# Moving operands whose places go round modulo 512 bytes: attention and two MLPs on one core

## The chip, the cores and the metric

The kernel runs on 1 core of a Trainium2 chip. The metric is the time of one execution on the device in microseconds; the kernel before has a median of 899.9 us over 3 runs (899.09 to 900.56).

## The reference

Attention over 4 batches, 8 heads, 576 positions of 64 elements, with a local mask (32 positions back) for heads 0 to 3 and a strided mask (every 32nd position) for heads 4 to 7, and then two MLPs over the 2304 tokens with 512 features and 2048 hidden ones. In short:

```
scores = q @ k.T / 8, masked;  attn = softmax(scores);  o = attn @ v
x = o as (2304, 512)
for w_in (512, 2048), w_out (2048, 512) of two layers:
    h = maximum(x @ w_in, 0)
    x = (h * h) @ w_out
```

All inputs and outputs are float32.

## The kernel before

**Operands in two parts.** TensorE multiplies in its fast float32 format. So every large operand is split into a high part and a rest (`hi` written by ScalarE, `lo = src - hi` by VectorE), and a product is made of three matmuls: hi by hi, hi by lo, lo by hi. Weights arrive as 64-bit words and are converted on VectorE and ScalarE while the first layer runs; attention's small matmuls are spread between those of the first three blocks.

**Blocks and steps.** The tokens of a layer are cut in five blocks (`BLOCKS`): four of 512 tokens (wide) and one of 256 (narrow). The narrow one is the fourth of the first layer and the first of the second. A step `s` takes one block and 128 hidden features (`f`), or two times 128 for a narrow block. So the first layer has 72 steps, of which 48 to 55 are narrow, and the second has 72, of which 72 to 79 are narrow. In step `s` TensorE runs the first product of step s+1 (`mm1`, line 704) and then the second product of step `s` (`mm2`, line 766, or for wide blocks of the second layer `products`, line 889).

**Which operand moves.** A matmul holds one operand still (stationary, loaded by a weight load) and streams the other through (moving, up to 512 columns).
- `mm1` (L704): w_in is stationary, x moves: 12 matmuls of 512 columns in a wide step, 24 of 256 in a narrow one. x of a block lies in the tiles `xh` and `xl`, four rows `c` of 512 floats each.
- `mm2` of the first layer (L766): w_out is stationary, g = relu(h) squared moves, from the tiles `gh` and `gl`: 12 matmuls of 512 columns or 24 of 256. In the narrow block of the second layer g is stationary and w_out moves, 12 matmuls of 512 columns.
- `products` (L889), wide blocks of the second layer: seven Strassen products over 256-wide halves. A pair of steps (f even and f odd) works on one set of operands. Combinations of g are stationary (`gah`, `gal`, `gbh`, `gbl`), combinations of w_out move, 256 columns each. The latter lie in a ring over the free x tiles, seven halves of 256 floats, which `w_operands` writes: first three (`PA`), then four (`PB`). A pair has 18 matmuls of the first three and 24 of the other four.

**Where they lie.** In the built program's layout the tiles of x, of the weights and of g (moving and stationary) all begin 128 bytes past a multiple of 512; the tile `gap` is there to bring this about. In this text a place is an operand's distance from that, modulo 512 bytes. Before the change every moving operand of L704 is at place 0, that of L766 at place 0 for wide blocks and 192 (48 floats) for the first layer's narrow block, that of L889 at 192.

**What sets the order.** The program is recorded in the order in which the code calls its operations (`manual_schedule`); each engine runs its own list in that order and waits on semaphores for the others.

Of the kernel before, what the change touches and what calls it, by code (L numbers as in the profile page):

```python
# [16 lines left out]
P = 128  # L17
B, H, S, D = 4, 8, 576, 64
STRIDE = 32
# [6 lines left out]
TB = 512  # L26
# [34 lines left out]
HALF = DM // 2  # L61
# [82 lines left out]
def r32(ap):  # L144
    return ap.bitcast(F32)
# [3 lines left out]
def tile_attention_then_two_mlps(  # L149
# [139 lines left out]
    def ready(key):  # L289
        while key not in wt:  # L290
            conv_by(1)
        return wt[key]
# [227 lines left out]
    def one_small():  # L520
        if small:
            small.pop(0)()
# [21 lines left out]
    def turn_x(i):  # L544
# [3 lines left out]
        for g in range(ng):  # L548
# [3 lines left out]
                ident[:nq, :nq],  # L552
            )

    def x_parts(i):

        b, u, kind, f = fills[i]
        ps = x_ps[i]
        parts = []
        if kind == "l":  # L560
            c = u
            t0, t1 = b * S + f * LQ, b * S + (f + 1) * LQ
            for j, (b0, nb) in enumerate(BLOCKS[0]):
                lo, hi = max(t0, b0), min(t1, b0 + nb)
                if lo < hi:
                    parts.append((j, ps[:, lo - t0:hi - t0], lambda x, a=lo - b0, e=hi - b0: x[:, c, a:e]))
        else:
            c = 2 + u
            r0, n, ng = SFILLS[f]
            n *= ng  # L570
            src = ps[:, :n * NPOS].rearrange("p (r i) -> p i r", i=NPOS)
            i0 = b * NPOS
            for j, (b0, nb) in enumerate(BLOCKS[0]):
                b0, nb = b0 // STRIDE, nb // STRIDE
                lo, hi = max(i0, b0), min(i0 + NPOS, b0 + nb)
                if lo < hi:
                    parts.append((
                        j,
                        src[:, lo - i0:hi - i0],
                        lambda x, a=lo - b0, e=hi - b0: x[:, c].rearrange(  # L580
                            "p (i r) -> p i r", r=STRIDE)[:, a:e, r0:r0 + n],
                    ))
        return parts
# [69 lines left out]
    blocks = [(layer, j) for layer in range(2) for j in range(NB)]  # L653

    def tiles_of(k):
        layer, j = blocks[k]
        return TB // BLOCKS[layer][j][1]
# [3 lines left out]
    xin = {}  # L661
# [9 lines left out]
    def split_y(k, c):  # L671
        layer, j = blocks[k]
        n = BLOCKS[layer][j][1]
        h, lo = (x[:, c, :n] for x in xin[k])
        t = y_in.pop((k, c))[:, :n]
        nc.scalar.activation(out=h, in_=t, func=AF.Copy)
        nc.vector.tensor_tensor(out=lo, in0=t, in1=r32(h), op=ALU.subtract)
# [3 lines left out]
    def block_x(k):  # L681
        layer, j = blocks[k]
        return (xh[j], xl[j]) if layer == 0 else xin[k]

    def mm1(s, point):

        if s >= len(steps):
            return
        k, f = steps[s]
        ne = tiles_of(k)  # L690
        n = TB // ne
        x_hi, x_lo = block_x(k)
        if s == first_7 + 1 or s != 1 and s < first_7 and n_att[0] == len(att):
            ps = ps_a.tile([P, TB], F32, tag="a", name="ps_h")
        elif s != 1:
            ps = ps_h.tile([P, TB], F32, tag="h", name="ps_h")
        else:
            ps = ps_a.tile([P, TB], F32, tag="a", name="ps_h")
        for c in range(KC):
            for e in range(ne):  # L700
                w = ready(("in", blocks[k][0], f + e))
                for i, (a, x) in enumerate(((0, x_hi), (0, x_lo), (1, x_hi))):

                    nc.tensor.matmul(  # L704
                        ps[:, e * n:(e + 1) * n],
                        lhsT=w[:, a, c * P:(c + 1) * P],
                        rhs=x[:, c, :n],
                        start=c == 0 and e == 0 and i == 0,
                        stop=c == KC - 1 and i == 2 and e == ne - 1,
                    )  # L710
                    one_small()
            if c < KC - 1:
                point()
        if s >= first_7:
            t = sqs[s] = gpool.tile([P, TB], F32, tag=("r", "sq")[s % 2], name="sq", bufs=1)
            nc.scalar.activation(out=t, in_=ps, func=AF.Relu, scale=W_BACK)  # L716
            nc.vector.tensor_tensor(out=t, in0=t, in1=t, op=ALU.mult)  # L717
            return

        g0 = 48 if ne > 1 and blocks[k][0] == 0 else 0  # L720
        r = gpool.tile([P, TB], F32, tag="r", name="r", bufs=1)
        sq = gpool.tile([P, TB], F32, tag="sq", name="sq", bufs=1)
        nc.scalar.activation(out=r, in_=ps, func=AF.Relu, scale=W_BACK)  # L723
        h = gpool.tile([P, TB + P], F32R, tag="gh", name="gh", bufs=2)[:, g0:g0 + TB]
        lo = gpool.tile([P, 3 * HALF], F32R, tag="gl", name="gl", bufs=2)[:, g0:g0 + TB]
        if 0 < n_load[0] - n_part[0]:

            nc.scalar.activation(out=sq, in_=r, func=AF.Square)
            nc.scalar.activation(out=h, in_=sq, func=AF.Copy)  # L729
        else:  # L730
            nc.scalar.activation(out=h, in_=r, func=AF.Square)
            nc.vector.tensor_tensor(out=sq, in0=r, in1=r, op=ALU.mult)  # L732
        nc.vector.tensor_tensor(out=lo, in0=sq, in1=r32(h), op=ALU.subtract)  # L733
        gh[s], gl[s] = h, lo
# [57 lines left out]
    sqs, ga, gb, w_parts, rings, banks = {}, {}, {}, {}, {}, {}  # L792
# [3 lines left out]
    def ring(n):  # L796

        if n not in rings:
            rings[n] = [x_tile(t, n).rearrange("p c n -> p (c n)") for t in ("xh", "xl")]
        return rings[n]  # L800
# [14 lines left out]
    def w_operands(s, first):  # L815

        k, f = steps[s]
        n = 1 if k == len(blocks) - 1 and f % 4 == 1 else 2
        wr = w_parts[s] = [x[:, 48:48 + 7 * HALF] for x in ring(n)]
        w = ready(("out", 1, f - 1)), ready(("out", 1, f))  # L820
        src, a, e = (w[0][:, 0:3], 0, 3) if first else (w[1], 3, 7)
        hi, lo = (x[:, a * HALF:e * HALF] for x in wr)
        parts(hi, lo, src.rearrange("p i m -> p (i m)"))

    def quarters(s):
# [43 lines left out]
    def products(s, which, point):  # L869
        k, f = steps[s]  # L870
        nt = TB // 2 // P
        first, end = f == 1, f == NF - 1
        wr = w_parts[s]
        (h, lo), names, w0 = (ga.pop(s), PA, 0) if which == 0 else (gb.pop(s), PB, 3)
        if first:
            tags = ("y0", "y1", "y2") if which == 0 else ("y3", "a", "a", "a")
            for name, tag in zip(names, tags):
                pool = ps_a if tag == "a" else ps_y
                banks[name] = pool.tile([P, 512], F32, tag=tag, name="ps_y")

        at = ((0, 2, 1) if first else (0, 1, 2)) if which == 0 else (2, 0, 3, 1)
        for i in at:
            y = banks[names[i]]
            cols = slice((w0 + i) * HALF, (w0 + i + 1) * HALF)
            for t in range(nt):
                rows = slice(t * P, (t + 1) * P)
                for m, (a, w) in enumerate(((h, wr[0]), (h, wr[1]), (lo, wr[0]))):

                    nc.tensor.matmul(  # L889
                        y[:, t * HALF:(t + 1) * HALF],  # L890
                        lhsT=a[:, i, rows],
                        rhs=w[:, cols],
                        start=first and t == 0 and m == 0,
                        stop=end and t == nt - 1 and m == 2,
                    )
            point()
            if end:
                sums(k, names[i])
# [65 lines left out]
    first = {k: steps.index((k, 0)) for k in range(NB, 2 * NB)}  # L964
    y_at = {}
    for k, s in first.items():

        s, lag, each = (first[NB], 2, 1) if k == NB + 1 else (s - 12, 3, 2)
# [7 lines left out]
    with tc.manual_schedule():  # L976
# [3 lines left out]
        ps = ps_h.tile([P, TB], F32, tag="h", name="ps_w")[:, :P]  # L980
# [18 lines left out]
        for s in range(len(steps)):  # L999
            k, f = steps[s]  # L1000
            layer, j = blocks[k]
# [5 lines left out]
            def point(s=s, layer=layer, j=j, f=f):  # L1007
                n_pt[0] += 1
                at = N_PT * s + n_pt[0]
                for b, (p0, p1) in enumerate(spans):  # L1010
                    if at > p0:
                        lo, hi = att_end[b], att_end[b + 1]
                        att_to(min(hi, lo + -(-(hi - lo) * (at - p0) // (p1 - p0))))
                if n_part[0] < half1:
                    conv_by(1 if n_pt[0] % 4 else 2)
                elif j == NB - 1 and f > 2 and layer == 0 or layer == 1 and n_pt[0] % 4:
                    conv_by(1)
# [3 lines left out]
            if s != first_7:  # L1021
                mm1(s + 1, point)
# [47 lines left out]
```

## Time and profile before

| | |
|---|---|
| median of 3 runs | 899.9 us |
| lowest, highest | 899.09, 900.56 us |
| span of the profiled execution | 896.8 us |
| granted TensorE clock, mean over the span | 0.993 |
| TensorE busy | 876.6 us (98%) in 5216 matmul instructions |
| weight loads busy | 765.4 us (85%) |
| VectorE busy | 631.2 us (70%) |
| ScalarE busy | 491.5 us (55%) |

The span runs from the first to the last instruction; the time of a run also holds what lies around it. Matmuls are pipelined: each is recorded from its start until its last result is written, which overlaps the next ones. How closely they follow each other is read from the chain of waits in order of time, where consecutive matmuls of one line are merged into a piece: its length divided by its count is the spacing. By stage: attention fills the first 40 us alone; the first layer's blocks run from 41 to 155, 157 to 266, 268 to 373, 375 to 418 (narrow) and 420 to 505 us; the second layer's from 507 to 550 (narrow), 552 to 631, 633 to 715, 717 to 799 and 801 to 883 us (Strassen), and a tail ends at 896.8.

### The profile page before, as it was taken

To read this page: it belongs to the slowest core of one execution; us is meant where nothing else is said; L and a number is where in the kernel's file an instruction comes from. 1 tells how busy PE (TensorE), PEld (TensorE's weight loads), DVE (VectorE), ACT (ScalarE), POOL (GpSimd) and SP (SyncE) were. 2 spreads that over 40 slices of the span, in tenths; PEclk is the share of its full clock that TensorE was granted. 3 is DMA by queue.
4 is the path that set the end of the run, shared out by engine and by line. 5 is a ranking of instruction groups with operands and counts; after the bars stand their busy time and mean duration, and the time that the engine had idled before them with its cause. 6 is when DMAs were issued, how large, how long until landed. Compare 5 with 4: busy or idle time off the path is not lost.

```text
span 896.8 us, 14022 instructions
## 1 busy us (share of the span) xinstructions
PE 876.6 (98%) x5216; PEld 765.4 (85%) x5216; DVE 631.2 (70%) x1521; ACT 491.5 (55%) x987; POOL 0.2 (0%) x4
## 2 busy tenths in 40 slices
PE   9699999999999999999999999999999999999997
PEld 8578878888888888899888898899989989998996
DVE  6999973477665665322299996777777787778676
ACT  6787863455555454322377794555545555554443
POOL 0000000000000000000000000000000000000000
PEclk9799999999999999999999999999999999999999
DMA  8956510222222220010566530100010020001001
GB/s 258 344 197 216 196 42 19 86 76 72 88 76 82 75 65 12 1 48 5 184 201 204 179 121 1 48 12 13 18 55 24 1 72 1 24 1 48 1 1 48
DMA packets 45939, 72.00 MB, mean 80 GB/s; under 512 B 3504, under 2 KB 32304, under 8 KB 45872
## 3 DMA queue, kind: packets, MB, share of 16 engines
q1 hardware_dynamic: 45872, 71.12, 24.0%
q8 instruction: 41, 0.67, 0.3%
q14 instruction: 26, 0.21, 0.1%
HBM read 61.67 MB, written 9.44 MB: 79 GB/s over the span
## 4 chain that ended last, share of the span: by engine, by line
PE 82%; DVE 14%; issue 2%; ACT 2%; DVEq 0%; ACTq 0%
PE ps_h L704 39%; PE ps_y L766 21%; PE ps_y L889 15%; DVE raw L223 2%; PE ps_o L503 2%; DVE val L234 2%; DVE w L268 2%; PE ps_pt L487 1%; DVE o L909 1%; PE ps_s L351 1%; DVE raw L220 1%; DVE s L464 1%; PE ps_s L444 1%; DVE gl L733 1%; PE ps_x L549 1%
## 5 line engine op out<-in xcount | busy, mean ns | idle before, releaser
L704 PE MATMUL ps_h<-xh,w 128*128 128x512 f32 (+1 forms) x1280 | 401.9, 374 | 0.0
L704 PEld LDWEIGHTS ps_h<-xh,w 128*128 128x128 f32 x1280 | 234.0, 189 | 36.2
L704 PE MATMUL ps_h<-xl,w 128*128 128x512 f32 (+1 forms) x640 | 236.4, 369 | 0.0
L766 PE MATMUL ps_y<-gh,w 128*128 128x512 f32 (+1 forms) x640 | 157.5, 376 | 0.0
L704 PEld LDWEIGHTS ps_h<-xl,w 128*128 128x128 f32 x640 | 121.3, 189 | 15.0 <-DVE xl L591 0.2
L766 PEld LDWEIGHTS ps_y<-gh,w 128*128 128x128 f32 x640 | 108.0, 188 | 16.5 <-ACT gh L729 0.2
L723 ACT ACTIVATE r<-ps_h 128x512 f32<-128x512 f32 x80 | 47.7, 596 | 122.4 <-PE ps_h L704 85.2
L732 DVE TENSOR_TENSOR sq<-r 128x512 f32<-128x512 f32 x50 | 34.6, 692 | 103.3 <-ACT r L723 103.3
L831 DVE TENSOR_TENSOR xl<-wf,xh 128x768 fp32r<-128x768 f32 (+1 forms) x80 | 80.0, 1010 | 18.5 <-ACT xh L830 18.2
L766 PE MATMUL ps_y<-gl,w 128*128 128x512 f32 (+1 forms) x320 | 85.4, 374 | 0.0
L830 ACT ACTIVATE xh<-wf 128x768 fp32r<-128x768 f32 (+1 forms) x80 | 68.9, 880 | 25.2 <-PE ps_y L889 25.2
L717 DVE TENSOR_TENSOR sq<-sq 128x512 f32<-128x512 f32 x64 | 44.1, 689 | 53.4 <-ACT sq L716 53.4
L716 ACT ACTIVATE sq<-ps_h 128x512 f32<-128x512 f32 x64 | 37.9, 593 | 72.5 <-PE ps_h L704 69.3
L889 PE MATMUL ps_y<-xl,gbh 128*128 128x256 f32 x256 | 72.1, 282 | 0.9 <-DVE xl L831 0.9
L889 PE MATMUL ps_y<-xh,gbl 128*128 128x256 f32 x256 | 71.9, 281 | 0.2 <-DVE gbl L831 0.2
L889 PE MATMUL ps_y<-xh,gbh 128*128 128x256 f32 x256 | 71.8, 281 | 0.0
L733 DVE TENSOR_TENSOR gl<-sq,gh 128x512 fp32r<-128x512 f32 x80 | 55.3, 691 | 20.5 <-ACT gh L729 14.6
L766 PEld LDWEIGHTS ps_y<-gl,w 128*128 128x128 f32 x320 | 54.5, 188 | 8.6
L480 ACT ACTIVATE s<-s,m 96x128 f32<-96x128 f32 (+2 forms) x176 | 55.7, 387 | 5.4 <-DVE m L464 4.8
L889 PE MATMUL ps_y<-xl,gah 128*128 128x256 f32 x192 | 54.0, 281 | 0.2 <-DVE xl L831 0.2
L889 PE MATMUL ps_y<-xh,gah 128*128 128x256 f32 x192 | 54.2, 282 | 0.0
L889 PE MATMUL ps_y<-xh,gal 128*128 128x256 f32 x192 | 54.0, 281 | 0.0
(77 smaller groups left out, 1347.2 us busy)
## 6 DMA issues: line engine op xcount, KB each, us to landing
raw<-moe_w_in_d SPq DMA_DIRECT2D x32, 512.0 KB, 4.7
raw<-moe_w_out_d SPq DMA_DIRECT2D x32, 512.0 KB, 3.8
qk<-loc_qk_d SPq DMA_DIRECT2D x12, 416.0 KB, 3.1
out_d<-o SPq DMA_DIRECT2D x18, 256.0 KB, 2.4
y_dram<-o SPq DMA_DIRECT2D x16, 256.0 KB, 2.1
y_in<-y_dram SPq DMA_DIRECT2D x16, 256.0 KB, 3.0
qk<-loc_qk_d SPq DMA_DIRECT2D x12, 304.0 KB, 3.6
v<-loc_v_d SPq DMA_DIRECT2D x24, 130.0 KB, 2.7
```

What stands on the lines that cost most here:

```text
L223: nc.vector.scalar_tensor_tensor(out=lower, in0=upper, scalar=-(2 ** 31), in1=lower, op0=ALU.bitwise_and, op1=ALU.bitwise_or)
L480: nc.scalar.activation(out=blk, in_=blk, func=AF.Exp, scale=-1.0, bias=m[:nq, j:j + 1])
L704: nc.tensor.matmul(ps[:, e * n:(e + 1) * n], lhsT=w[:, a, c * P:(c + 1) * P], rhs=x[:, c, :n], start=c == 0 and e == 0 and i == 0, stop=c ...
L716: nc.scalar.activation(out=t, in_=ps, func=AF.Relu, scale=W_BACK)
L717: nc.vector.tensor_tensor(out=t, in0=t, in1=t, op=ALU.mult)
L723: nc.scalar.activation(out=r, in_=ps, func=AF.Relu, scale=W_BACK)
L732: nc.vector.tensor_tensor(out=sq, in0=r, in1=r, op=ALU.mult)
L733: nc.vector.tensor_tensor(out=lo, in0=sq, in1=r32(h), op=ALU.subtract)
L766: nc.tensor.matmul(y, lhsT=lhsT, rhs=rhs, start=f == 0 and c not in seen, stop=end and m == last[c])
L830: nc.scalar.activation(out=hi, in_=src, func=AF.Copy)
L831: nc.vector.tensor_tensor(out=lo, in0=src, in1=r32(hi), op=ALU.subtract)
L889: nc.tensor.matmul(y[:, t * HALF:(t + 1) * HALF], lhsT=a[:, i, rows], rhs=w[:, cols], start=first and t == 0 and m == 0, stop=end and t == ...
```

## The change

The moving operands get other starting places inside their tiles. `x_at` gives each of the four rows of a narrow block's x a shift of its own: 0, 64, 96 and 128 floats in the first layer, 16, 32, 80 and 112 in the second (wide blocks fill their rows and stay). g of step `s` begins 16 x (s modulo 8) floats into its tile in both layers before the Strassen blocks, where it began at 48 for the first layer's narrow block and at 0 elsewhere. Strassen's operands of w_out begin at 16 x (s // 2 modulo 8) floats for the pair of step `s`, where they began at 48; their last four halves lie 128 floats further on than the first three would have them, which leaves the place modulo 512 bytes as it is. 16 floats are 64 bytes, so eight shifts go once round 512 bytes. The changed kernel issues the same instructions in the same order on every engine, with the same waits; starting addresses alone differ.

```diff
--- before.py
+++ after.py
@@ -552,6 +552,12 @@
                 ident[:nq, :nq],
             )
 
+    def x_at(layer, n, c):
+
+        if n == TB:
+            return 0
+        return ((0, 64, 96, 128), (16, 32, 80, 112))[layer][c]
+
     def x_parts(i):
 
         b, u, kind, f = fills[i]
@@ -563,7 +569,7 @@
             for j, (b0, nb) in enumerate(BLOCKS[0]):
                 lo, hi = max(t0, b0), min(t1, b0 + nb)
                 if lo < hi:
-                    parts.append((j, ps[:, lo - t0:hi - t0], lambda x, a=lo - b0, e=hi - b0: x[:, c, a:e]))
+                    parts.append((j, ps[:, lo - t0:hi - t0], lambda x, a=lo - b0, e=hi - b0, o=x_at(0, nb, c): x[:, c, o + a:o + e]))
         else:
             c = 2 + u
             r0, n, ng = SFILLS[f]
@@ -571,13 +577,14 @@
             src = ps[:, :n * NPOS].rearrange("p (r i) -> p i r", i=NPOS)
             i0 = b * NPOS
             for j, (b0, nb) in enumerate(BLOCKS[0]):
+                o = x_at(0, nb, c)
                 b0, nb = b0 // STRIDE, nb // STRIDE
                 lo, hi = max(i0, b0), min(i0 + NPOS, b0 + nb)
                 if lo < hi:
                     parts.append((
                         j,
                         src[:, lo - i0:hi - i0],
-                        lambda x, a=lo - b0, e=hi - b0: x[:, c].rearrange(
+                        lambda x, a=lo - b0, e=hi - b0, o=o, nb=nb: x[:, c, o:o + nb * STRIDE].rearrange(
                             "p (i r) -> p i r", r=STRIDE)[:, a:e, r0:r0 + n],
                     ))
         return parts
@@ -671,7 +678,8 @@
     def split_y(k, c):
         layer, j = blocks[k]
         n = BLOCKS[layer][j][1]
-        h, lo = (x[:, c, :n] for x in xin[k])
+        o = x_at(layer, n, c)
+        h, lo = (x[:, c, o:o + n] for x in xin[k])
         t = y_in.pop((k, c))[:, :n]
         nc.scalar.activation(out=h, in_=t, func=AF.Copy)
         nc.vector.tensor_tensor(out=lo, in0=t, in1=r32(h), op=ALU.subtract)
@@ -697,6 +705,7 @@
         else:
             ps = ps_a.tile([P, TB], F32, tag="a", name="ps_h")
         for c in range(KC):
+            x0 = x_at(blocks[k][0], n, c)
             for e in range(ne):
                 w = ready(("in", blocks[k][0], f + e))
                 for i, (a, x) in enumerate(((0, x_hi), (0, x_lo), (1, x_hi))):
@@ -704,7 +713,7 @@
                     nc.tensor.matmul(
                         ps[:, e * n:(e + 1) * n],
                         lhsT=w[:, a, c * P:(c + 1) * P],
-                        rhs=x[:, c, :n],
+                        rhs=x[:, c, x0:x0 + n],
                         start=c == 0 and e == 0 and i == 0,
                         stop=c == KC - 1 and i == 2 and e == ne - 1,
                     )
@@ -717,7 +726,7 @@
             nc.vector.tensor_tensor(out=t, in0=t, in1=t, op=ALU.mult)
             return
 
-        g0 = 48 if ne > 1 and blocks[k][0] == 0 else 0
+        g0 = 16 * (s % 8)
         r = gpool.tile([P, TB], F32, tag="r", name="r", bufs=1)
         sq = gpool.tile([P, TB], F32, tag="sq", name="sq", bufs=1)
         nc.scalar.activation(out=r, in_=ps, func=AF.Relu, scale=W_BACK)
@@ -816,10 +825,11 @@
 
         k, f = steps[s]
         n = 1 if k == len(blocks) - 1 and f % 4 == 1 else 2
-        wr = w_parts[s] = [x[:, 48:48 + 7 * HALF] for x in ring(n)]
+        w0 = 16 * (s // 2 % 8)
+        wr = w_parts[s] = [(x[:, w0:], x[:, w0 + P:]) for x in ring(n)]
         w = ready(("out", 1, f - 1)), ready(("out", 1, f))
         src, a, e = (w[0][:, 0:3], 0, 3) if first else (w[1], 3, 7)
-        hi, lo = (x[:, a * HALF:e * HALF] for x in wr)
+        hi, lo = (x[not first][:, a * HALF:e * HALF] for x in wr)
         parts(hi, lo, src.rearrange("p i m -> p (i m)"))
 
     def quarters(s):
@@ -889,7 +899,7 @@
                     nc.tensor.matmul(
                         y[:, t * HALF:(t + 1) * HALF],
                         lhsT=a[:, i, rows],
-                        rhs=w[:, cols],
+                        rhs=w[which][:, cols],
                         start=first and t == 0 and m == 0,
                         stop=end and t == nt - 1 and m == 2,
                     )
```

## Rows read from the trace of the kernel before

**Rows 1.** The page: busy time by engine, and the chain that ended last.
```profile
PE 876.6 (98%) x5216; PEld 765.4 (85%) x5216; DVE 631.2 (70%) x1521; ACT 491.5 (55%) x987; POOL 0.2 (0%) x4
...
PE 82%; DVE 14%; issue 2%; ACT 2%; DVEq 0%; ACTq 0%
PE ps_h L704 39%; PE ps_y L766 21%; PE ps_y L889 15%; DVE raw L223 2%; PE ps_o L503 2%; DVE val L234 2%; DVE w L268 2%; PE ps_pt L487 1%; DVE o L909 1%; PE ps_s L351 1%; DVE raw L220 1%; DVE s L464 1%; PE ps_s L444 1%; DVE gl L733 1%; PE ps_x L549 1%
```

**Rows 2.** Busy time by stretch: start and end, length, engines, clock, DMA.
```profile
375.00:418.00 43.00, 43.00 (x356) 42.39 (x355) 10.15 (x17) 10.91 (x19) 0.00 (x0) 1.00 0.07 26
420.00:505.00 85.00, 85.00 (x390) 70.95 (x389) 62.88 (x122) 53.46 (x95) 0.00 (x0) 1.00 0.56 185
552.00:631.00 79.00, 78.78 (x478) 70.42 (x478) 55.27 (x93) 39.87 (x65) 0.00 (x0) 1.00 0.06 21
```

**Rows 3.** Chain in order of time, first narrow block and after: start, length, what.
```profile
381.32 2.87 PE ps_h L704 x24
384.19 2.74 PE ps_y L766 x24
...
414.93 2.86 PE ps_h L704 x24
417.79 2.74 PE ps_y L766 x24
420.53 2.73 PE ps_h L704 x12
423.27 2.83 PE ps_y L766 x24
426.09 2.72 PE ps_h L704 x12
428.81 2.72 PE ps_y L766 x12
```

**Rows 4.** The same chain in a Strassen block.
```profile
631.15 2.83 PE ps_y L889 x24
633.97 2.72 PE ps_h L704 x12
636.69 2.12 PE ps_y L889 x18
638.81 2.73 PE ps_h L704 x12
```

**Rows 5.** The same chain in the second layer's narrow block.
```profile
507.69 2.87 PE ps_h L704 x24
510.57 2.75 PE ps_y L766 x12
```

**Rows 6.** VectorE in L733 alone, wide and narrow block: busy time and count.
```profile
268.50:373.00 104.50, 10.39 (x15) 1.00 0.16 50
375.50:418.00 42.50, 4.85 (x7) 1.00 0.07 25
```

**Rows 7.** Chain in order of time, attention's score matmuls between others.
```profile
335.43 0.23 PE ps_s L351 x2
...
337.95 0.24 PE ps_s L351 x2
```

**Rows 8.** Timeline at 747.3 us, matmuls and then weight loads: start, length, engine, what.
```profile
747.32 0.28 PE L889 MATMUL ps_y<-xl,gbh 128*128 128x256 f32 x1
747.43 0.28 PE L889 MATMUL ps_y<-xh,gbl 128*128 128x256 f32 x1
...
747.32 0.19 PEld L889 LDWEIGHTS ps_y<-xh,gbl 128*128 128x128 f32 x1
```

## Prediction

> **What bounds the kernel now.** I read the page's first part: TensorE is busy 98% of the span, VectorE 70%, ScalarE 55% [rows 1]. A busy share of TensorE says little, so next came the chain that ended last: 82% of it is TensorE, and its three largest pieces are the lines that this change touches, L704 (first product of a layer, 39%), L766 (second product, 21%) and L889 (the seven Strassen products, 15%) [rows 1]. By stage, TensorE is busy 43.00 of 43.00 us in the narrow block, 85.00 of 85.00 in the block behind it and 78.78 of 79.00 in a Strassen block, where VectorE has 24 us to spare [rows 2]. The granted clock there is 1.00, the 2.4 GHz level. So from 157 us on the kernel lasts as long as its matmuls follow each other, and a nanosecond saved or lost on each of thousands of matmuls stands in the time. (A matmul's own duration, 281 or 389 ns in the rows by line, overlaps the next one; it is no spacing.)
>
> The spacing is read from the chain in order of time, whose pieces are whole steps: length by count. A piece of 512 columns at 2.4 GHz streams for 213.3 ns, one of 256 for 106.7. What the rows show [rows 3 to 5]:
> - wide, everything at place 0 (the kernel's tiles of x, weights and g all begin at the same place modulo 512 bytes): 2.72 us / 12 = 226.7 ns;
> - L704 narrow, place 0: 2.87 / 24 = 119.6 ns;
> - L766 narrow, moving operand 48 floats (192 bytes) on: 2.74 / 24 = 114.2 ns in seven steps, but 2.83 / 24 = 117.9 in the eighth, which follows a wide L704 instead of a narrow one;
> - L889, also 192 bytes on: 2.83 / 24 = 117.9, 2.12 / 18 = 117.8 in every block.
>
> So the spacing differs by up to 5.4 ns between operands that differ in place alone, and at one place there are two spacings, by what ran before. That is all that the change can act on.
>
> **The change part by part.** No instruction is added, dropped or put elsewhere on any queue, and each waits for what it waited for: the second half of Strassen's operands of w_out is moved by 128 floats (L866's call) just so that a later first half at a larger shift does not touch it. The DMAs go where they went. ScalarE and VectorE write the moved operands in the same shapes; L733 takes 4.85 / 7 = 693 ns writing 192 bytes on and 10.39 / 15 = 693 ns at place 0 [rows 6], so a place costs the writer nothing, and the slack above would cover it if it did. What is left is the spacing of matmuls, in five groups.
>
> 1. *L889*, 1344 matmuls, 42 in each of 32 pairs of steps. The place is now 64 bytes times (s // 2 % 8): of 32 pairs, 4 stay at 192, 4 are at 0, 24 at the six other places. At place 0 I take 119.6 (the narrow L704 row): 4 x 42 x 1.7 ns = +0.3 us. For the six others the trace has no steady row. Bounds: 114.2, the lowest narrow spacing, gives 1008 x -3.7 ns = -3.7 us; one more step of 5.4 ns above 119.6, so 125, gives 1008 x 7.1 = +7.2 us. The nearest row is L351, also 256 columns, whose operands stand at many places (its groups begin 96, 108 or 126 floats apart): 0.23 to 0.24 us for two, 115 to 120 ns each [rows 7]. I take 118.8, between the two steady values for those places not known to be good: +0.9 us.
> 2. *L704 narrow*, 2 blocks x 8 steps x 24 = 384 matmuls at 119.6. In layer 0 two of four rows of x stay at place 0 modulo 512 (shifts 0 and 128 floats): 96 matmuls unchanged. The other 288 go to 118.8: -0.2 us. Bounds as above: 114.2 gives -1.6, 125 gives +1.6 us.
> 3. *L766 narrow*, 8 steps x 24. Seven of eight leave the place that gave 114.2: 168 x 4.6 = +0.8 us. Bounds 0 and, at 125, +1.8 us.
> 4. *L766 wide*, layer 0: 64 steps x 12 matmuls at 226.7, of which 56 steps leave place 0. Its steady spacing elsewhere is in no row; a fall or rise as between the two narrow values, 5.4 ns on 672 matmuls, bounds it at -3.6 and +3.6 us. What the rows do show is that a wide group at place 0 behind a differing one takes a while to come back to 226.7: 2.75 instead of 2.72 behind each narrow group of the second layer, 2.73 behind the 114.2 spacing [rows 3, 5]. From now on x (place 0) and g (place 1 to 7) alternate in 56 steps; 0.03 us each would be +1.7. Since L889 at 192 alternates with x at 0 and L704 stays at 2.72 to 2.73 there [rows 4], I take half: +0.8 us.
> 5. *Stationary g* of the layer-2 narrow block (shift 16 x (s % 8) where it was 0): 7 groups of 12, each already 2.75 [rows 5]. Nothing taken; with group 4's bound 0.5 us either way.
>
> Sum: 0.3 + 0.9 - 0.2 + 0.8 + 0.8 = +2.6 us. The profiled execution's span is 896.8 us, the median of the runs 899.9, so 3.1 us lie around the span; with the change 896.8 + 2.6 = 899.4 span and 902.5 us. The head (before 157 us) and the tail after 883 us hold none of it.
>
> A rule that speaks against any effect: the row shows one line, one shape, at one clock spaced 114.2, 117.9 [rows 3], so something besides the column count enters. The Trainium skill (SBUF — State Buffer, "SBUF: two separate sides" and the part on the bandwidth-pool intuition) says that TensorE has its own port, with a second independent one for loading weights, and never waits on anyone in SBUF; by that a place is worth nothing and the sum is 0. The trace does not agree within L766, but does not prove that the place is the reason.
>
> **The rivals.**
> - *R1, the place does not matter* (the spacing follows from what ran before, as the 114.2 and 117.9 at one place hint). For it: those two rows. Against it: L704 at place 0 and L766 at 192 alternate in one block and stay 5.4 ns apart, in the same shape. Time: 899.9 us. This is also the case in which the change does not do what it says, and the one that the named rule gives.
> - *R2, most other places are better than the present ones* (faster). The mechanism: the weight load of the next matmul starts with the present one, at 747.32 us both [rows 8], and where both read the same place modulo 512 at once, one is held up; place 0 is then the worst, and 192 only half out of the way. L889 and L704 narrow fall to 114.2 wherever they are moved, except 0: 1008 x -3.7 - 288 x 5.4 = -5.3 us, with 4 x 42 matmuls at place 0 giving back 0.3; wide L766 gains half of its bound, -1.8; L766 narrow stays. Together -6.8: 893.1 us; with half of the places good, 897. For it: 119.6 against 114.2. Against: L351's many places average no better than 118, and the wide spacing has shown nothing below 226.7. It decides from the point where more than half of the unknown places read under 117.9.
> - *R3, a step higher*: some places cost another 5.4 ns above 119.6 for narrow and as much for wide. Half of the bounds of groups 1 to 4: 3.6 + 0.8 + 0.9 + 1.8 = +7.1, so 907 us. For it: disturbed groups already run above their steady value (2.75 against 2.72). Against: no whole narrow group in the trace is above 2.87.
>
> **How the numbers follow.** Forecast 0.48, R1 0.14, R2 0.25, R3 0.13. The forecast's own range is 900 to 905.5. 0.2% (1.8 us) is about what a measurement of this kernel can tell from no change; so faster means below 898.1 and slower above 901.7. The forecast case gives slower 0.36, same 0.10, faster 0.02; R1 same 0.13, slower 0.01; R2 faster 0.22, same 0.03; R3 slower 0.13. Together faster 0.24, same 0.26, slower 0.50. The range that holds 8 in 10 reaches to half of R2 and to R3: 895.5 to 908.5.
>
> **What would show it.** In the chain of the changed kernel the L889 pieces of 24 should no longer all be 2.83 but differ step by step with a period of eight pairs, 2.83 where the shift is 48 floats and near 2.87 where it is 0; L766 narrow should mostly be above 2.74; wide L766 at 2.72 for s % 8 = 0 and 2.73 to 2.77 elsewhere, L704 wide behind it likewise. If all L889 pieces stay 2.83, R1 holds; if most are 2.74, R2. The forecast is wrong if wide L766 has its own steady spacing at other places, below 2.70 or above 2.78, for with 768 matmuls that outweighs the rest; or if VectorE or ScalarE shows up between steps of a Strassen block.

## The result and the profile after

The changed kernel takes 905.66 us (median of 3 runs, 904.46 to 905.68) against 899.9: a ratio of 1.0057 with a 95% interval of 1.0037 to 1.0077, so 3.3 to 6.9 us slower (5.1 by the ratio, 5.8 by the medians). The profiled execution's span is 903.8 us, 7.0 more than before; part of that is what single executions differ by, as shown below.

The page first: the same counts, nearly the same shares, TensorE 98% [rows 1]. TensorE is busy 4.9 us longer with as many matmuls; the page does not say where.

```profile
span 903.8 us, 14022 instructions
...
PE 881.5 (98%) x5216; PEld 766.7 (85%) x5216; DVE 631.9 (70%) x1521; ACT 492.3 (54%) x987; POOL 0.2 (0%) x4
```

The chain in order of time says where (start, length, what; the diff moves L704, L766 and L889 to L713, L775 and L899). In the first layer's narrow block the L775 pieces of 24 go round with a period of four steps. 2.73 comes once, at 48 floats, where seven pieces had 2.74; four steps on, at 112 floats, the piece follows a wide L713 and has 2.83 (426.39), as the eighth piece of before had. In the last wide block of that layer the first five steps show 2.72 at shifts 0 and 64 floats (431.94 and 453.98) and 2.76, 2.79, 2.80 between, with L713 behind them at 2.77, 2.73, 2.74 [rows 3].

```profile
383.89 2.85 PE ps_h L713 x24
386.74 2.88 PE ps_y L775 x24
...
392.47 2.83 PE ps_y L775 x24
...
398.15 2.84 PE ps_y L775 x24
...
403.83 2.73 PE ps_y L775 x24
...
426.39 2.83 PE ps_y L775 x24
429.22 2.72 PE ps_h L713 x12
431.94 2.72 PE ps_y L775 x12
...
437.38 2.76 PE ps_y L775 x12
440.14 2.77 PE ps_h L713 x12
442.92 2.79 PE ps_y L775 x12
445.71 2.73 PE ps_h L713 x12
448.44 2.80 PE ps_y L775 x12
451.24 2.74 PE ps_h L713 x12
453.98 2.72 PE ps_y L775 x12
```

In a Strassen block the pieces of 18 and 24 are 2.12 and 2.83 at 48 floats (599.49, 604.33), as before, 2.12 and 2.83 at 16 floats too (578.47, 583.35), 2.16 and 2.88 at 32 (588.93, 593.85), and 2.15 and 2.87 at 64 (609.88, 614.78); but the L713 pieces behind them are 2.72 only at 48, 2.76 at 16 and 32, and 2.75 at 64 [rows 4].

```profile
578.47 2.12 PE ps_y L899 x18
580.59 2.76 PE ps_h L713 x12
583.35 2.83 PE ps_y L899 x24
...
588.93 2.16 PE ps_y L899 x18
591.09 2.76 PE ps_h L713 x12
593.85 2.88 PE ps_y L899 x24
...
599.49 2.12 PE ps_y L899 x18
601.62 2.72 PE ps_h L713 x12
604.33 2.83 PE ps_y L899 x24
...
609.88 2.15 PE ps_y L899 x18
612.03 2.75 PE ps_h L713 x12
614.78 2.87 PE ps_y L899 x24
```

Set against the same pieces of before, the second narrow L704 group comes 2.57 us late (383.89 for 381.32), the wide L704 behind the block 3.13 (429.22 for 426.09), and each Strassen block adds 0.8 us by its pieces. Not all of the 2.57 is the change's. In the run below in which Strassen's operands alone go round, and so nothing is moved before the second layer, the same group comes 1.44 us late:

```profile
382.76 2.87 PE ps_h L704 x24
```

The loss that the pieces show lies in the steps whose operands went round, a little in most of them.

### The profile page after: what moved, and what is told of

Its sections match the earlier page's. It is cut to its first block, busy times and chain, and to the rows that moved or that the text cites. A ratio compares the mean times of both kernels' runs of the same rounds, so it can differ in the third digit from the quotient of the medians.

```text
span 903.8 us, 14022 instructions
## 1 busy us (share of the span) xinstructions
PE 881.5 (98%) x5216; PEld 766.7 (85%) x5216; DVE 631.9 (70%) x1521; ACT 492.3 (54%) x987; POOL 0.2 (0%) x4
## 4 chain that ended last, share of the span: by engine, by line
PE 82%; DVE 13%; ACT 2%; issue 1%; DMA 1%; SPq 0%; DVEq 0%; ACTq 0%
PE ps_h L713 40%; PE ps_y L775 21%; PE ps_y L899 15%; PE ps_o L503 2%; DVE raw L223 2%; DVE w L268 2%; DVE val L234 2%; PE ps_pt L487 1%; PE ps_s L351 1%; DVE o L919 1%; DVE raw L220 1%; DVE s L464 1%; DMA qk<-st_qk_d 1%; DVE gl L742 1%; PE ps_s L444 1%
## 5 line engine op out<-in xcount | busy, mean ns | idle before, releaser
L713 PE MATMUL ps_h<-xh,w 128*128 128x512 f32 (+1 forms) x1280 | 403.6, 375 | 0.0
L713 PEld LDWEIGHTS ps_h<-xh,w 128*128 128x128 f32 x1280 | 234.1, 189 | 38.2 <-ACT r L732 0.2
L713 PE MATMUL ps_h<-xl,w 128*128 128x512 f32 (+1 forms) x640 | 237.1, 371 | 0.0
L775 PE MATMUL ps_y<-gh,w 128*128 128x512 f32 (+1 forms) x640 | 158.9, 378 | 0.0
L713 PEld LDWEIGHTS ps_h<-xl,w 128*128 128x128 f32 x640 | 121.2, 189 | 15.6
L775 PEld LDWEIGHTS ps_y<-gh,w 128*128 128x128 f32 x640 | 108.4, 188 | 17.2
L775 PE MATMUL ps_y<-gl,w 128*128 128x512 f32 (+1 forms) x320 | 86.2, 376 | 0.0
L899 PE MATMUL ps_y<-xl,gbh 128*128 128x256 f32 x256 | 72.4, 283 | 0.9 <-DVE xl L841 0.9
L899 PE MATMUL ps_y<-xh,gbl 128*128 128x256 f32 x256 | 72.3, 282 | 0.2 <-DVE gbl L841 0.2
L899 PE MATMUL ps_y<-xh,gbh 128*128 128x256 f32 x256 | 71.9, 281 | 0.0
L775 PEld LDWEIGHTS ps_y<-gl,w 128*128 128x128 f32 x320 | 54.8, 188 | 9.1
L899 PE MATMUL ps_y<-xl,gah 128*128 128x256 f32 x192 | 54.2, 282 | 0.2 <-DVE xl L841 0.2
L899 PE MATMUL ps_y<-xh,gah 128*128 128x256 f32 x192 | 54.2, 282 | 0.0
L899 PE MATMUL ps_y<-xh,gal 128*128 128x256 f32 x192 | 54.2, 282 | 0.0
```

What stands on the lines that cost most here:

```text
L713: nc.tensor.matmul(ps[:, e * n:(e + 1) * n], lhsT=w[:, a, c * P:(c + 1) * P], rhs=x[:, c, x0:x0 + n], start=c == 0 and e == 0 and i == 0, ...
L775: nc.tensor.matmul(y, lhsT=lhsT, rhs=rhs, start=f == 0 and c not in seen, stop=end and m == last[c])
L899: nc.tensor.matmul(y[:, t * HALF:(t + 1) * HALF], lhsT=a[:, i, rows], rhs=w[which][:, cols], start=first and t == 0 and m == 0, stop=end a ...
```

## The experiments

In all of them the kernel before is run on the same chip beside them; ratios are with 95% intervals. The kernel of places alone, further down, was run once, and its trace is what counts. Theory A: the spacing follows the distance between the moving and the stationary operand's places modulo 256 bytes, and the next group settles for some matmuls (its spacing takes a few matmuls to become steady). Theory E, added later: one place has two spacings, and what ran before chooses.

### Three parts of the change, each alone

Wide g alone:

```diff
-        g0 = 48 if ne > 1 and blocks[k][0] == 0 else 0
+        g0 = (48 if ne > 1 else 16 * (s % 8)) if blocks[k][0] == 0 else 0
```

> Only g of the first layer's wide blocks goes round (16 x (s % 8) floats); x of narrow blocks, Strassen's operands and g of narrow blocks stay where they were. Theory A (the spacing follows the distance between the moving operand's place and the stationary one's, modulo 256 bytes, and a following group at another place settles for some matmuls): from the pieces of the changed kernel, L766 wide costs +3.6, +6.0, +6.7, 0, +3.6, +6.0, +6.7 ns per matmul at 64 to 448 bytes, 96 matmuls each, +3.1 us, and the settling of the L704 groups behind it +1.4 us: +4.5 us, 904.4 us. Rival B (the wide operand adds half a settling per step as forecast, the rest of the measured loss lies in Strassen's blocks): +0.8 us, 900.7 us.

Measured: 901.36 us, 1.0017 (1.0008 to 1.0025), +1.5 us. That is between the two numbers given; the interval takes in rival B's +0.8 us and leaves out theory A's +4.5. The rows say why, and that A is right where nothing disturbs the steps. In the block from 427.91 to 510.51 its pieces are those of the changed kernel, and the block takes 1.0 us more than before (82.60 for 81.60, [rows 3, 5]), as theory A has it for two rounds of eight steps. But all three earlier wide blocks together and the head bring 1.82 us in this one execution (383.14 for 381.32), of which, by the 1.44 us above, most may be no more than the difference of two executions.

```profile
269.97 2.73 PE ps_h L704 x12
...
383.14 2.87 PE ps_h L704 x24
...
427.91 2.72 PE ps_h L704 x12
...
510.51 2.86 PE ps_h L704 x24
```

In those blocks attention's small matmuls stand between every few of the large ones, and there the kernel before has no steady spacing either. Its chain has a whole step of 12 at 268.69, and behind it pieces of three that are 227 to 240 ns a matmul:

```profile
268.69 2.72 PE ps_h L704 x12
...
280.67 0.72 PE ps_y L766 x3
...
288.44 0.68 PE ps_h L704 x3
```

I had multiplied the steady difference by all 64 steps; from the third wide block's second step (269.97 for 268.69) to the narrow block it cost 0.5 us, not 1.1. That attention's matmuls are the reason is my reading; no run leaves them out.

Strassen's operands alone:

```diff
-        wr = w_parts[s] = [x[:, 48:48 + 7 * HALF] for x in ring(n)]
+        w0 = 16 * (s // 2 % 8)
+        wr = w_parts[s] = [(x[:, w0:], x[:, w0 + P:]) for x in ring(n)]
...
-        hi, lo = (x[:, a * HALF:e * HALF] for x in wr)
+        hi, lo = (x[not first][:, a * HALF:e * HALF] for x in wr)
...
-                        rhs=w[:, cols],
+                        rhs=w[which][:, cols],
```

> Only Strassen's operands of w_out go round (16 x (s // 2 % 8) floats). Theory A: direct, 168 matmuls at each place, +1.9 ns at 0 and 256 bytes, +2.0 at 128 and 384, +0.1 at 64 and 320, 0 at 192 and 448: +1.4 us; settling of the L704 groups behind them, 96 matmuls at each place, +2.3 ns (0, 256), +3.0 (64, 320), +3.7 (128, 384), 0 (192, 448): +1.7 us; together +3.1 us, 903.0 us. Rival B (the loss is all Strassen's): +5 us, 905 us. If A holds in both, this one and the one for wide g add up to more than the whole change, whose narrow x then gives some 1 us back.

Measured: 903.01 us, 1.0032 (1.0021 to 1.0043), +2.9 us by the ratio. Theory A's size, and well under the rival's 5.

The narrow rest alone (from the changed kernel, wide g back to 0, Strassen back to 48):

```diff
-        g0 = 16 * (s % 8)
+        g0 = 16 * (s % 8) if ne > 1 else 0
...
-        w0 = 16 * (s // 2 % 8)
+        w0 = 48
```

> The rest of the change alone: narrow x and g of narrow blocks (moving in the first layer, stationary in the second) go round as in the changed kernel; g of wide blocks stays at 0 and Strassen's operands at 192 bytes. Theory A, from the changed kernel's pieces: L704 narrow -0.5, L766 narrow +0.6, the second layer's 12 wide matmuls with shifted g +0.3: +0.4 us, 900.2 us. Rival (what is missing between 1.5 + 3.2 us of the two parts and the whole change's 5.8 lies here): +1.1 us, 900.9 us.

Measured: 899.96 us beside 899.53, 1.0005 (0.9996 to 1.0014): +0.4 us. The interval takes in no change, theory A's +0.4 us and the rival's +1.1, so the time decides nothing here. The three parts add up to 1.5 + 2.9 + 0.4 = 4.8 us of the whole change's 5.1.

### Which places are alike

> Only change: g of the first layer's wide blocks lies 64 floats (256 bytes) on, in every step. Theory A (modulo 256 bytes): every piece of L766 wide stays 2.72 us, no settling, 899.9 us. Rival C (modulo 512 bytes; the changed kernel's pieces at 256 look good only by where they stand in the order): L766 wide has the far place in all 64 steps and L704 settles behind it, +2 to +6 us, 902 to 906 us.

```diff
-        g0 = 48 if ne > 1 and blocks[k][0] == 0 else 0
+        g0 = (48 if ne > 1 else 64) if blocks[k][0] == 0 else 0
```

Measured: 899.47 us, 0.9995 (0.9986 to 1.0004). 256 bytes are as good as 0, in all 64 steps; rival C is out.

> Only change: a pad of 48 floats (192 bytes) ahead of the weights, so that weights, x, g and Strassen's operands, moving and stationary, all lie 192 bytes further on and their distances stay. Theory A (distance between moving and stationary): no change, 899.9 us, pieces 2.72, 2.83 and 2.87 as before. Rival D (the moving operand's own place modulo 256): all wide matmuls at the place that costs +6.7 ns, 1536 of L704 and 768 of L766, +15 us, and L889 at 128 instead of 192, +2 ns on 1344, +2.7 us: about 918 us.

```diff
+    ctx.enter_context(tc.tile_pool(name="pad", bufs=1)).tile([P, 48], F32, name="pad")
     wpool = ctx.enter_context(tc.tile_pool(name="weights", bufs=1))
```

Measured: 899.9 us, 0.9996 (0.9987 to 1.0005). Rival D asked for 918. With everything 192 bytes on, the distance counts, not the place.

### The spacing by itself

A kernel of its own, all of whose matmuls stand on one line. VectorE is idle in it; ScalarE copies each group's result out (54.6 us busy of 359), and DMAs store it; the granted clock is 1.00 in those 359 us:

```python
for i, (n, xp, wp) in enumerate(seq):        # columns, moving place, stationary place (bytes)
    nc.tensor.matmul(ps[:, :n], lhsT=w[:, wp // 4 + i % 8 * P:wp // 4 + (i % 8 + 1) * P],
                     rhs=x[:, xp // 4:xp // 4 + n], start=i == 0, stop=i == len(seq) - 1)
```

> Leaves the whole computation out: TensorE alone runs groups of matmuls with no other engine beside them, 12 wide ones at place 0 between any two groups. Groups of 24 wide (512 columns) and of 24 narrow (256) at every place from 0 to 480 bytes by 32, stationary at 0; narrow at each place behind six narrow ones at place 0 (kick); wide with the stationary operand shifted (held), with both shifted alike (both), and alternating by 192 bytes in step (in_step: each matmul's own two operands agree, the next weight load differs) and out of step (out_step: its own differ, the next weight load agrees). Theory A: period 256; wide 226.7 ns at 0 and 256, 230 to 233 elsewhere; narrow near 119.6 at 0 and 256, 117.8 at 64 and 192 (and 320, 448), 119.8 at 128; both = 226.7 at every shift; held as moving with the sign turned. If what collides is the next weight load with the running stream, out_step stays at 226.7 and in_step does not; if a matmul's own operands matter, the reverse. Theory E (two states at one place, chosen by what ran before): the kick at 192 gives 113.3 after a few matmuls where the group behind wide ones gives 117.8. Rival F (the spacings come from VectorE and ScalarE working beside): no place differs from another here.

The chain in order of time, one piece per group; the name tells place and width (w wide, n narrow). Groups have 24, `between` 12, `kick` 30 of which the first six are at 0.

```profile
20.89 5.44 PE at0w L39 x24
...
37.41 5.51 PE at64w L39 x24
42.92 2.77 PE between L39 x12
...
54.06 5.59 PE at128w L39 x24
...
70.74 5.60 PE at192w L39 x24
...
87.42 5.44 PE at256w L39 x24
92.86 2.72 PE between L39 x12
...
153.96 2.87 PE at0n L39 x24
156.83 2.75 PE between L39 x12
...
187.58 2.83 PE at192n L39 x24
190.41 2.72 PE between L39 x12
...
198.73 2.87 PE at256n L39 x24
...
262.48 3.45 PE kick192n L39 x30
...
293.82 5.60 PE held64w L39 x24
...
326.89 5.49 PE held192w L39 x24
...
335.10 5.45 PE both192w L39 x24
...
359.64 7.41 PE in_step L39 x32
...
369.77 7.46 PE out_step L39 x32
```

The numbers of the kernel are all here without VectorE, and with ScalarE busy 15% instead of 55%: wide 226.7 ns at 0 and 256, 229.6 at 64, 233 at 128 and 192; narrow 119.6 at 0 and 256, 117.9 at 192. So rival F is out. Odd multiples of 32 bytes, not quoted, are 233.3 to 234.2 for wide; for narrow, 32 and 288 bytes take 2.80 a piece, less than any multiple of 64 behind wide matmuls, and the others 2.84 to 2.88. Shifting the stationary operand by 64 acts as shifting the moving one by 192 (5.60 both), by 192 as by 64 (5.49 and 5.51), and shifting both by 192 gives 5.45: theory A once more. (Shifting both by 64, not quoted, gives 5.48: its first ten matmuls settle, and the rest are at 226.7.) `between` shows the settling: the same twelve matmuls at place 0 take 2.72 behind a wide group at 0 or 256 and a narrow one at 192 or 448, and 2.73 to 2.77 behind every other group whose moving operand alone is shifted, and behind a narrow one at 0 or 256. The kick is theory E: 30 matmuls in 3.45 us where six at 119.6 and 24 at 117.9 would take 3.55. Whether fewer matmuls, or other places ahead, do the same was not tried.

Which of the two reads meet, the running matmul's with its own weight load or with the next one, did not come out: both ways of alternating by 192 bytes are slow, 7.41 / 32 = 231.6 and 7.46 / 32 = 233.1 ns. Neither reading fits alone, and that stays open.

### Choosing the state

Where narrow x takes its shift is as in the change itself (`x_at` and its calls), with another table. If a short stay at place 0 lets narrow matmuls at 192 run at 113.3 ns, the kernel before can be made faster.

```diff
+    def x_at(layer, n, c):
+        return 48 if n < TB and c else 0
```

> From the kernel before: rows 1 to 3 of narrow x 48 floats (192 bytes) on, row 0 left at place 0. Theory E: the six matmuls at place 0 at the head of every L704 narrow group bring the other 18 to 113.3 ns after some four, so a piece of 24 takes 2.77 to 2.78 us in place of 2.87, 16 groups, -1.5 us: 898.3 us. Rival G (192 bytes gives 117.8 whatever ran before): 18 x -1.8 ns per group, -0.5 us, 899.3 us.

Measured: 898.24 us, 0.9987 (0.9978 to 0.9996). The interval reaches rival G's -0.5 us as well as theory E's -1.5; the pieces decide for E, since by G a narrow L704 piece would take 2.84. In its trace a narrow step of the first layer is 2.76 and 2.72 us long, where 2.87 and 2.74 stood [rows 3]:

```profile
392.50 2.76 PE ps_h L711 x24
395.26 2.72 PE ps_y L773 x24
```

In Strassen's blocks W_AT gives each half's start, `w_operands` writes to it in two pieces, and the operands of the two first products (at 0 and 1344 floats) lie at place 0:

```diff
+W_AT = (0, 304, 560, 816, 1072, 1344, 1648)
...
-            cols = slice((w0 + i) * HALF, (w0 + i + 1) * HALF)
+            cols = slice(W_AT[w0 + i], W_AT[w0 + i] + HALF)
```

> From the kernel before: in each half of a pair of Strassen steps the first product's operand of w_out lies at place 0, the others stay at 192 bytes; w_operands writes each half in two pieces instead of one (64 more instructions on ScalarE and 64 on VectorE, beside TensorE's work). Theory E: six matmuls at place 0 (some 118 each), four to come down, then 113.3 ns: pieces of 24 take 2.76 in place of 2.83 and of 18 2.07 in place of 2.12, less 0.01 us for L704 behind each: -3.0 us, 896.8 us. Rival G (192 bytes gives 117.8 whatever ran before): six matmuls in each group at 119 instead of 117.8, +0.5 us, 900.3 us.

Measured: 897.09 us, 0.9972 (0.9963 to 0.9981): theory E, where rival G asked for a small loss.

> Both edits: narrow x as in v1_narrow_x and Strassen's first products at place 0 as in v2_kick. Theory E: -1.5 - 3.0, 895.3 us. Rival G: 899.8 us.

Measured: 895.68 us, 0.9960 (0.9947 to 0.9972): 3.6 us less than before by the ratio, where 4.5 were expected, and the fastest of all here. Its Strassen pieces are 2.09 and 2.77 where 2.12 and 2.83 stood, with L704 at 2.73 behind [rows 4]:

```profile
583.30 2.09 PE ps_y L902 x18
585.39 2.73 PE ps_h L713 x12
588.12 2.77 PE ps_y L902 x24
```

## Why the prediction was right, and where it was thin

The forecast was slower, 902.5 us, by a mixture of spacings; measured 905.66, in the range of 895.5 to 908.5 and just over the forecast's own 900 to 905.5. The direction and the kind of cause were right. The size was about half of what came, +2.6 us for 5.1, and it lies in a range 13 us wide by some luck: the prediction's own sign of being wrong is in the chain, wide pieces above 2.78 (2.79 and 2.80), and had the other wide blocks gone like the undisturbed one, they would have added nearly 3 us more, up to the edge of the range. By its steps:

- **What bounds the kernel**: right. In the chains read the pieces follow each other without a gap, and their spacing carries the loss.
- **Step 1, L889**: forecast +1.2 us. By the pieces, +0.03, +0.04 at 0, nothing at 64 and 192, +0.04, +0.05 at 128, twice round in each of four blocks: +1.3 us. The value 118.8 held as a mean, though no place has it: 119.6 and 119.8 at half of them and 117.9 at the other half.
- **Steps 2 and 3, narrow L704 and L766**: forecast -0.2 and +0.8; the pieces give -0.5 and +0.65, and the part alone measured +0.4 together with step 5, for which nothing was taken and the pieces give +0.2.
- **Step 4, wide L766**: the term that was mis-sized. I took only a settling, halved, +0.8 us. Wide groups have steady spacings of their own, 229.6 to 233.3 ns, which the trace before could not show; alone the step cost +1.5. It would have been 4.3 at the undisturbed block's rate, over all 64 steps. (The first 16 of them lie between 41 and 155 us: that the head before 157 us holds none of the sum does not fit with counting 64.)
- **The settling of L704 behind L889**: the term that was missing. I cited that L704 stays 2.72 behind L889 at 192 as a reason to halve the settling; but 192 is, with 448, the one place of Strassen's eight behind which it does not settle. Behind the others the pieces are 0.03 to 0.04 us longer, 1.8 us in the four blocks.

Of the rivals, R1 (place without effect) fell with the parts measured alone: with no more than a copy beside TensorE, one shape at one clock is spaced from 226.7 to 234 ns by the distance of its operands. But its hint was half of the truth: at one place there are two spacings, 113.3 and 117.8, by what ran before; the 114.2 of the prediction's row is 113.3 with a few settling matmuls ahead. The distances also speak against the rule of the Trainium skill that the prediction set beside R1 (SBUF — State Buffer, "SBUF: two separate sides"), that TensorE never waits on anyone in SBUF; the measurement decides. R2 named the right kind of cause, distance, and the wrong direction: 192 for Strassen, with the group behind it, and 0 for wide are the best of the eight (448 and 256 are as good), and only narrow x stood badly. R3, at 907, came nearer to the time than the forecast, in part by another way: wide matmuls do go up by 6.7 ns, but no narrow piece shown is above 2.88. And the period I foretold, eight pairs, is four.

## What to carry to other kernels

Where matmuls follow each other without a gap, read their spacing from whole pieces of the chain, and look at moving and stationary operands' addresses modulo 256 bytes: here equal for 512 columns, and for 256 columns 192 apart in its faster state, was best of what was tried, worth up to 3% of a wide matmul and 6% of a narrow one. A steady state can depend on what ran before, so a place is judged by its group and by the group behind it, and a few matmuls at another place can choose the better state. A number taken from undisturbed steps should not be multiplied by disturbed ones.

## What the hardware showed that I had not expected

Distances that differ by 256 bytes give the same times to the hundredth of a microsecond in pieces of 24 (0 and 256: 5.44 and 5.44, 2.87 and 2.87), at every multiple of 32 bytes that the kernel of places alone went through. And narrow matmuls 192 apart have two steady spacings, 117.8 and 113.3 ns, each of which holds to the end of its group of 24; six matmuls at distance 0 ahead move them from the slower to the faster.
